# Chunk attention, expert layer, expert layer: chunk form for all attention, wider first loads, and a queue change

## The chip, the cores and the metric

The kernel runs on one core of a Trainium2 chip (trn2). A core has TensorE (matmuls into PSUM, with a weight load of its own), VectorE, ScalarE and GpSimd (called POOL in the profile), and SyncE, which only issues transfers. Each engine runs its own instructions in order; semaphores join them. The metric is the device time of one execution in microseconds; of several runs the median is taken.

## The reference, cut to what matters

```
q, k, v: (4, 8, 768, 64); mem_k, mem_v: (4, 8, 8, 64); float32, q, k and mem_k scaled up
for c in range(24):                       # chunks of 32 queries
    k_ctx = k[:, :, max(0, 32c-16) : min(768, 32c+32+8)]     # v_ctx alike
    scores = (q_c @ concat(mem_k, k_ctx).T) / 8
    a = softmax(scores)                   # subtracts the row's maximum
    out_c = a @ concat(mem_v, v_ctx)
x = out as (3072, 512)
h = x @ w_in (512, 2048); g = h * tanh(log1p(exp(h)));  x = g @ w_out (2048, 512)
h = x @ w_in2;            g = h / (1 + exp(-1.702 h));  y = g @ w_out2
```

The two expert layers have their own weights. The kernel gets arrays as 64-bit floats where they are weights, so a weight arrives as two 32-bit words and is made into one f32 on the chip.

## The kernel before, in words

The 3072 tokens are eight blocks of 384 (`j` = 0 to 7), two for each batch item. For each block attention gives xT, the layer's input with features on partitions; then 16 forward products, one for each slice `f` of 128 hidden columns (L1218), whose results are taken out of PSUM (L1350, L1351) and written to DRAM. Layer 1's second half and layer 2 follow with staged products (seven products in place of eight for each 2 x 2 of halves), into which the change does not reach. From block 1 on every product is three fp32r matmuls (high by high, low by high, high by low); block 0's forward is one plain f32 matmul for each 128 features, because there are no split weights yet.

Attention of blocks 0 and 1 (`EARLY = 2`) is in a windowed form: 96 queries against 120 keys of their neighbourhood and 8 memory keys at a time, with a mask of -3e38 outside each chunk's own keys. `rows_of_heads` loads q, k and v for all eight heads in 256-byte pieces, most of them on SyncE's queue; `turned` has TensorE turn q and k (L761), `quad` makes scores and softmax (L829 to L880), `quad_out` or `oct_out` turns the exponentials (L911, L991) and multiplies by v (L928, L1013). Block 0 is done before the first forward product, block 1 between the forwards of block 0.

Attention from block 2 on is in chunk form: `pair_of_heads` loads q and k for two heads in 128-byte pieces and turns them on VectorE in 32 x 32 squares (L669, L672), `values_of` loads v on POOL's queue, and `duo` does four heads at once: chunk by chunk, 32 queries by 64 keys (8 memory keys among them), scores at L1054, softmax at L1068 to L1088, turn at L1096, values at L1116, and the evictions into xh and xl at L1128 and L1132. Block j's attention stands among the forwards of block j-1.

Layer 1's first weight comes in 16 loads of 0.5 MB, one for each f, in 1-KB pieces (`w_conv`, `w_first`). Each is made into f32 by a drop of the low words (L416 on ScalarE or L419 on VectorE), a shift (L425), a low word (L429) and a sign (L433), and is split into high and low later (`w_cut`; L529, L534).

No engine's order is written by hand. A `Plan` collects operations with a rank and a modelled duration for each engine that could do them, and `issue` lists them in the order of its own modelled time; ties go by rank. So the ranks (`rank`, `base`, `LEAD`, `AHEAD`, `CUT`) and modelled prices (`bus`, the numbers in `load`) set each engine's order and each queue's when the kernel is built. A tile is released when its last reader is done; `Shared`, `Spread` and `Part` place small tiles within large ones.

## Time and profile before

| | us |
|---|---|
| runs before, median of 3 | 1103.59 (1102.69 to 1104.82) |
| the profiled execution, its own time | 1105.13 |
| its span in the trace | 1103.3 |
| TensorE busy | 1079.3 (98%) |
| VectorE busy | 800.3 (73%) |
| ScalarE busy | 555.8 (50%) |
| POOL busy | 98.6 (9%) |
| mean granted TensorE clock, of full speed | 0.998 |

The profile is of one execution. Busy times are of the span; the 1.8 us between span and time lie around the program. PEld is TensorE's weight load, which runs beside its matmuls, and SPq, POOLq and so on are an engine's sequencer, which issues transfers and waits. TensorE is busy almost all the time after the first 40 us, so an average over the span tells little: the stages have to be looked at one by one.

### The profile page before, as it was taken

The page shows a single profiled execution, that of the slowest core. Times are in us where ns is not written, and L with a number is a line of the kernel's source. Part 1 is how long each engine was busy: PE and PEld are TensorE (multiplying, and loading weights), DVE is VectorE, ACT ScalarE, POOL GpSimd, SP SyncE. Part 2 cuts the span into 40 slices and gives each one's busy share as a digit, 9 for nine tenths or more (in the row PEclk, how much of TensorE's full clock was granted, in tenths as well). Part 3 has the DMA queues.
Part 4 walks back from the last instruction along what each step waited for, and adds up shares of the span by engine and source line. Part 5 has one row for each costly group of instructions (what it writes and reads, how often), then busy time and mean ns, then how long its engine had stood idle before and what let it go on. Part 6 is the DMA issues. An engine that isn't in the chain of part 4 may idle for free.

```text
span 1103.3 us, 24808 instructions
## 1 busy us (share of the span) xinstructions
PE 1079.3 (98%) x9642; PEld 1041.1 (94%) x9642; DVE 800.3 (73%) x1456; ACT 555.8 (50%) x1246; POOL 98.6 (9%) x169
## 2 busy tenths in 40 slices
...
GB/s 172 264 241 189 242 247 228 205 250 268 278 276 222 249 175 147 216 212 121 189 172 86 208 260 223 296 227 290 203 265 261 160 106 166 112 133 145 105 165 46
DMA packets 278733, 221.28 MB, mean 201 GB/s; under 512 B 113553, under 2 KB 253868, under 8 KB 278616
## 3 DMA queue, kind: packets, MB, share of 16 engines
...
q14 instruction: 42, 0.34, 0.1%
HBM read 138.33 MB, written 81.26 MB: 199 GB/s over the span
## 4 chain that ended last, share of the span: by engine, by line
PE 78%; DMA 10%; DVE 5%; SPq 4%; issue 1%; ACT 1%; DVEq 0%; ACTq 0%
PE o L1481 9%; PE o L1573 9%; PE h L1218 9%; PE o L1218 8%; PE h L1380 7%; PE o L1380 6%; PE s L1481 6%; PE h L1573 6%; PE h L1481 6%; PE s L1573 5%; SPq L375 4%; PE s L1380 3%; DMA st<-wd 3%; DMA st<-in_moe_w_out_dram 2%; DMA g1d<-ev 1%
## 5 line engine op out<-in xcount | busy, mean ns | idle before, releaser
L1218 PE MATMUL h<-xh,wi 128*128 128x384 f32 x320 | 82.9, 340 | 0.0
L1218 PE MATMUL o<-xh,wi 128*128 128x384 f32 x320 | 82.7, 339 | 0.0
L1218 PEld LDWEIGHTS h<-xh,wi 128*128 128x128 f32 x320 | 57.2, 188 | 0.6
L1218 PEld LDWEIGHTS o<-xh,wi 128*128 128x128 f32 x320 | 57.0, 188 | 0.5
L1218 PE MATMUL h<-xl,wi 128*128 128x384 f32 x160 | 53.7, 336 | 0.0
L1218 PE MATMUL o<-xl,wi 128*128 128x384 f32 x160 | 53.7, 336 | 0.0
L1350 ACT ACTIVATE e<-h 128x384 f32<-128x384 f32 (+2 forms) x47 | 22.4, 477 | 45.4 <-PE h L1573 28.8
L1573 PE MATMUL o<-wo,xh 128*128 128x256 f32 x232 | 43.7, 282 | 0.0
L1563 DVE TENSOR_TENSOR xl<-vt,xh 128x1024 fp32r<-128x1024 f32 x24 | 29.3, 1223 | 19.7 <-ACT xh L1560 18.0
L1563 DVE TENSOR_TENSOR xl<-wi,xh 128x1024 fp32r<-128x1024 f32 x32 | 38.8, 1222 | 5.9 <-ACT xh L1560 5.1
L1481 PE MATMUL o<-xh,wo 128*128 128x256 f32 x224 | 40.5, 282 | 0.0
L1560 ACT ACTIVATE xh<-wi 128x1024 fp32r<-128x1024 f32 x25 | 26.4, 1056 | 23.0 <-DMA wi<-gd 12.4
L375 POOL DMA_DIRECT2D vt<-in_v_dram x50 | 32.2, 648 | 63.3 <-PE o L1116 33.6
L375 POOL DMA_DIRECT2D wo<-in_v_dram x50 | 31.7, 638 | 53.7 <-PE o L1116 51.1
L1464 DVE TENSOR_TENSOR xl<-z,xh 128x1024 fp32r<-128x1024 f32 x24 | 29.2, 1222 | 9.7 <-ACT xh L1460 9.1
L1218 PE MATMUL o<-wo,wi 128*128 128x384 f32 x192 | 36.2, 340 | 0.0
L1573 PEld LDWEIGHTS o<-wo,xh 128*128 128x128 f32 x232 | 36.0, 190 | 0.0
L1218 PE MATMUL h<-wo,wi 128*128 128x384 f32 x192 | 35.7, 339 | 0.0
L1481 PEld LDWEIGHTS o<-xh,wo 128*128 128x128 f32 x224 | 34.6, 190 | 0.0
L1218 PEld LDWEIGHTS h<-wo,wi 128*128 128x128 f32 x192 | 33.2, 188 | 0.2
L1218 PEld LDWEIGHTS o<-wo,wi 128*128 128x128 f32 x192 | 33.0, 188 | 0.4
L1350 ACT ACTIVATE ev<-o 128x384 f32<-128x384 f32 (+2 forms) x31 | 14.5, 469 | 36.7 <-PE o L1573 17.5
...
## 6 DMA issues: line engine op xcount, KB each, us to landing
...
```

What stands on the lines that cost most here:

```text
L375: queue.dma_start(out=o, in_=i)
L1218: nc.tensor.matmul(out=h.get(), lhsT=a[:, c], rhs=b.at(kk), start=(n == 0), stop=(n == KD * len(prods) - 1))
L1350: ("act", act(n, True), lambda: nc.scalar.activation(out=dst(), in_=bank.get(), func=AF.Copy)),
L1380: nc.tensor.matmul(out=bank.get(), lhsT=a, rhs=b, start=(fresh and m == 0), stop=(m == 3 * K2 - 1), skip_group_check=not fresh,)
L1464: add(rank + 0.05, [("dve", dve(n2), lambda gh=gh, gl=gl, src=src: nc.vector.tensor_tensor(out=flat(gl), in0=flat(src), in1=flat(gh), op=A ...
L1481: nc.tensor.matmul(out=bank[:, d, :], lhsT=a, rhs=b[:, p, :], start=(fresh and h == d == p == m == 0), stop=(h == 1 and p == HP - 1 and m ...
L1560: ("act", act(NP * P), lambda: nc.scalar.activation(out=flat(gh), in_=flat(src), func=AF.Copy)),
L1563: add(rank + 0.05, [("dve", dve(NP * P), lambda: nc.vector.tensor_tensor(out=flat(gl), in0=flat(src), in1=flat(gh), op=ALU.subtract))], re ...
L1573: nc.tensor.matmul(out=bank.get(), lhsT=a[:, p], rhs=b, start=(fresh and p == 0 and m == 0), stop=(p == NP - 1 and m == 2), skip_group_che ...
```

## The change

All blocks use the chunk form; the windowed form, its masks and helpers go. Four more things change with it:

- Block 0's q and k come in 1-KB pieces (four rows of 64 floats), q on ScalarE's queue and k on SyncE's, and are turned by TensorE: eight matmuls of 64 x 96 (q) or 64 x 104 (k) with an identity for each pair of heads (L681), taken out of PSUM by strided copies (L695). `WIDE = 0` keeps block 1 on 128-byte pieces on SyncE.
- From block 2 on q's four transfers for each pair of heads go by POOL's queue (`via=NARROW`). v of all blocks does too. Memory values are loaded in even blocks alone, since the odd block finds them in place.
- Layer 1's first weight is loaded for two slices at once, half of the features at a time: still 16 loads of 0.5 MB, but in 2-KB pieces. `Joined` finds a slice's part in the two halves. The first product now needs the first two loads.
- Block 0's results are taken out of PSUM into three tiles in turn (`gh`, `gl`, `ev`), not two.

`attention(j)` is called once at the start of block j-1, its ranks start 4 slices ahead (12 from block 2 on, as before), and the modelled prices of transfers are new. After the change the lines are: drop L430 and L433, shift L439, low L443, sign L447, split L550 and L555; scores L788, softmax L802 to L822, turn L830, values L850, evictions L861 to L866; forward L901, its evictions L1033 and L1034.

```diff
 WARM = 16
-LEAD = 8
+NARROW = 0.64
 SOON = 12
+FIRST = 4
 AHEAD = 6
 CUT = 6
 URGENT = 4
 LANDING = 3.5
-STAGGER = 1.5
 LATE = 3
+WIDE = 0
+LEAD = 2
 TURN = 2.7
 VAL = 7.2
```

```diff
+class Joined:
+    def __init__(self, parts, f):
+        self.parts, self.f = parts, f
+    def __getitem__(self, kk):
+        per = 4 // len(self.parts)
+        part, at = self.parts[kk // per], (2 * (kk % per) + self.f) * 128
+        return part[:, at:at + 128]
```

```diff
-def bus(nbytes, run):
-    return nbytes / 290e3 * (1 if run >= 512 else 1.3 if run >= 256 else 1.8)
+def bus(nbytes, run, soft=False):
+    if soft:
+        return nbytes / 290e3 * (1.07 if run >= 256 else 1.45)
+    return nbytes / 290e3 * (0.8 if run == 2048 else 0.88 if run == 1536 else 1 if run >= 512 else 1.75 if run >= 256 else 1.93)
...
-    T.update(ql=Shared(z0, 0), kl=Shared(z0, TB), mem_t=Shared(z0, TB + 32 * NKB), qT=Shared(z1, 0), kT=Shared(z1, 448))
-    T.update(gh=Shared(z2, 0, TB), aT=Shared(z3, 0, TB))
+    T.update(gh=Shared(z2, 0, TB), aT=Shared(z3, 0, TB), mem_t=Shared(z0, TB + 32 * NKB))
     T.update(tags(ps, h=2, s0=1, s1=1, **{f"o{i}": 1 for i in range(4)}))
     for f in range(NF):
         T.update(tags(sb, **{f"{n}{f}": 1 for n in ("wi", "wo")}))
-    def load(rank, buf, parts, nbytes, run, reads=(), early=False, via=None):
+    w11, w12, w13, w14, w15 = (T[f"wo{i}"].new([P, 2 * DM], F32) for i in range(11, 16))
+    vs = [T["vt"].new([P, 2 * DM], F32) for _ in range(2)]
+    T["ql"] = Spread((z0, 0), (w13, 0))
+    T["kl"] = Spread((z0, TB), (w13, TB))
+    T["qT"] = Spread(*((z, 0) for z in (z1, w15, w11)))
+    T["kT"] = Spread(*((z, TB) for z in (z1, w15, w11)))
+    T["vh"] = Spread(*((z, 0) for z in (w12, w14, *vs)))
+    T["ml"] = Shared(w12, NCH * D)
+    early = [T[f"wi{i}"].new([P, 2 * DM], F32) for i in range(8, 16)]
+    for i, (n, at) in enumerate((("qT", 0), ("kT", TB), ("ql", 0), ("kl", DM))):
+        T[n + "0"] = Spread(*((z, at) for z in early[i // 2 * 4:i // 2 * 4 + 4]))
...
             def go(queue, part=part):
                 o, i = part()
                 queue.dma_start(out=o, in_=i)
 
-            size = bus(nbytes / len(parts), run)
-            ways = [
-                ("sp", 0.475, lambda go=go: go(nc.sync), size),
-                ("pool", 1.2, lambda go=go: go(nc.gpsimd), size),
-            ]
-            add(rank, [("pool", 0.8, *ways[1][2:])] if via else ways if early else ways[:1], reads=reads, writes=[buf])
+            way = ("sp", 0.475, lambda go=go: go(nc.sync), bus(nbytes / len(parts), run))
+            if on == "act":
+                way = ("act", 0.5, lambda go=go: go(nc.scalar), way[3])
+            elif via:
+                way = ("pool", via, lambda go=go: go(nc.gpsimd), bus(nbytes / len(parts), run, True))
+            add(rank, [way], reads=reads, writes=[buf])
```

```diff
-    def w_conv(layer, f, part, rank, after, v, st):
+    def w_conv(layer, f, part, rank, after, v, st, half=None):
         src = w_src[layer, part]
 
         begun.append(fixed())
-        pace_by = begun[-1 - AHEAD:-AHEAD] if (layer, part) == (1, 0) else []
+        pace_by = [] if half is None else begun[-1 - AHEAD:-AHEAD]
 
         st = T[st].new([P, 2 * DM], I32)
         if part == 0:
+            k, c = (KD, 2 * P) if half is None else (KD // 2, 4 * P)
             load(rank - 3, st, [lambda: (
-                st.get().rearrange("p (k c) -> p k c", k=KD),
-                src[:, f * 2 * P:(f + 1) * 2 * P].rearrange("(k p) c -> p k c", p=P),
-            )], P * 8 * DM, 1024, pace_by)
+                st.get().rearrange("p (k c) -> p k c", k=k),
+                src[(half or 0) * k * P:][:k * P, f * 2 * P:f * 2 * P + c].rearrange("(k p) c -> p k c", p=P),
+            )], P * 8 * DM, 4 * c, pace_by)
...
     def w_first(f):
-        if f % 2 == 0:
-            pairs.append(T[f"wo{f // 2}"].new([P, 2 * DM], F32))
-        wi[f] = Part(pairs[-1], f % 2 * DM, DM)
-        w_conv(1, f, 0, f - 1.5, (), wi[f], f"wi{f}")
+        whole = T[f"wo{f // 2}"].new([P, 2 * DM], F32)
+        halves = [Part(whole, i * DM, DM) for i in range(2)]
+        for i in range(2):
+            w_conv(1, f, 0, f - 1.5, (), halves[i], f"wi{f + i}", i)
+            wi[f + i] = (Joined(halves, i),)
 
     def w_cut(f):
-        v = wi[f]
-        wi[f] = split_words(f + CUT, T[f"wi{f}"].new([P, 2 * DM], F32R), 0, DM, v, v.get)
-    pairs = []
+        halves = wi[f][0].parts
+        both = [T[f"wi{f + i}"].new([P, 2 * DM], F32R) for i in range(2)]
+        words = list(zip(*(split_words(
+            f + CUT, [Part(t, i * DM, DM) for t in both], v, v.get) for i, v in enumerate(halves))))
+        for i in range(2):
+            wi[f + i] = [Joined(w, i) for w in words]
```

```diff
+    def wide_pair(j, hp, rank):
+        n, few = 4, LEFT // 4
+        nq, nk = TB // n, NKB * CHUNK // n
+        ql = T["ql0"].new([P, 2, n, D], F32)
+        kl = T["kl0"].new([P, 2, n, D], F32)
+        own = "0" * (j == 0)
+        qT = T["qT" + own].new([P, TB], F32)
+        kT = T["kT" + own].new([P, NKB, BLK], F32)
+        r0 = 2 * hp * S + j * TB
+        k0 = few * (j == 0)
+        lead = LEAD if j else 4
+        load(rank - lead, ql, [lambda: (
+            ql[:nq].rearrange("p h r d -> p h (r d)"), rows(q, r0, [(n, nq), (S, 2)], 0, n * D)
+        )], 2 * TB * D * 4, 1024, on=None if j else "act")
+        if j == 0:
+            add(rank - 4.5, [("dve", 0.25, lambda: nc.vector.memset(kl[:few], 0.0))], writes=[kl])
+        load(rank - lead, kl, [lambda: (
+            kl[k0:nk].rearrange("p h r d -> p h (r d)"), rows(k, r0 + n * k0 - LEFT, [(n, nk - k0), (S, 2)], 0, n * D)
+        )], 2 * NKB * CHUNK * D * 4, 1024)
+        def turn(raw, m, t):
+            for r in range(n):
+                for hh in range(2):
+                    nc.tensor.matmul(
+                        out=t[hh * D:(hh + 1) * D, r * m:(r + 1) * m], lhsT=raw[:m, hh, r], rhs=ident[:m, :m],
+                        start=True, stop=True, tile_position=(0, hh * D),
+                    )
+        for raw, m, to in ((ql, nq, qT), (kl, nk, kT)):
+            t = T["h"].new([P, n * m], F32)
+            add(rank, [("pe", 0.45, lambda raw=raw, m=m, t=t: turn(raw, m, t))], reads=[raw, ident], writes=[t])
+            if to is qT:
+                o, i = qT.get().rearrange("p (t r) -> p t r", r=n), t.get().rearrange("p (r t) -> p t r", r=n)
+            else:
+                o = kT[:, :, :CHUNK].rearrange("p c (t r) -> p c t r", r=n)
+                i = t.get().rearrange("p (r c t) -> p c t r", r=n, t=CHUNK // n)
+            add(rank, [
+                ("act", act(n * m, True), lambda o=o, i=i: nc.scalar.activation(out=o, in_=i, func=AF.Copy)),
+                ("dve", dve(n * m), lambda o=o, i=i: nc.vector.tensor_copy(out=o, in_=i)),
+            ], reads=[t], writes=[to])
```

```diff
+        if j == 0 or j == 1 and hp < WIDE:
+            return wide_pair(j, hp, rank)
         ql = T["ql"].new([P, TB // 32, 32], F32)
         kl = T["kl"].new([P, NKB, 32], F32)
-        qT = T["qT"].new([P, 2 * (GQ + P)], F32)
+        qT = T["qT"].new([P, TB], F32)
...
+        load(rank - (LEAD if j == 1 else 4), ql, qs, P * TB * 4, 128, via=NARROW * (j > 1))
+        load(rank - (LEAD if j == 1 else 4), kl, ks, P * NKB * 128, 128)
         add(rank, [("dve", dve(TB), lambda: nc.vector.transpose(
-            out=qT[:, :TB], in_=ql.get().rearrange("p c d -> p (c d)")
+            out=qT.get(), in_=ql.get().rearrange("p c d -> p (c d)")
         ))], reads=[ql], writes=[qT])
         add(rank, [("dve", dve(NKB * CHUNK), lambda: nc.vector.transpose(out=kT[:, :, :CHUNK], in_=kl.get()))], reads=[kl], writes=[kT])
```

```diff
-            ))
-        load(rank, vt, parts, P * NCH * D * 4, 256, via="pool")
+            if s0 == 0:
+                parts.append(lambda row=i * D + CHUNK, h=h: (
+                    vt[row:row + NM], rows(mem_v, h * NM, [(1, NM), (0, NCH)], 0, D)
+                ))
+        load(rank, vt, parts, P * NCH * D * 4, 256, via=NARROW)
         return vt
...
-    def rows_of_heads(j, gp, rank):
...
-    def turned(j, hp, gp, st, rank):
...
-    def oct_scores(pairs, rank, names):
...
-    def quad(j, hp, gp, heads, rank, given=None, both=None):
...
-    def quad_out(j, hp, gp, vt, rank, names, e):
...
-    def oct_out(j, rank, vt, heads):
```

```diff
+    def attention(j):
+        s0 = j * TB % S
+        base = NF * (j - 1) - (FIRST if j == 0 else 4 if j == 1 else SOON)
+        if s0 == 0:
+            memory_keys(j * TB // S, base)
+        for hp in range(0, H // 2, 2):
+            r0 = base + 4 * hp
+            duo(j, hp, [pair_of_heads(j, hp + i, r0) for i in range(2)], r0)
...
-        ws1 = wi[f] if j else (wi[f],)
+        ws1 = wi[f]
...
                 a, b = ws1[0], x0[j][0]
...
-                        out=h.get(), lhsT=a[:, c], rhs=b.at(kk), start=(n == 0), stop=(n == KD * len(prods) - 1)
+                        out=h.get(), lhsT=a[kk], rhs=b.at(kk), start=(n == 0), stop=(n == KD * len(prods) - 1)
...
-        if j == 0:
-            w_cut(f)
-        t = T[("gh", "gl", "ev")[i % 3] if j else ("gh", "gl")[f % 2]].new([P, TB], F32)
+        if j == 0 and f % 2:
+            w_cut(f - 1)
+        t = T[("gh", "gl", "ev")[i % 3]].new([P, TB], F32)
...
+    attention(0)
     for j in range(NB):
         for f in range(NF):
-            if j == 0:
+            if j == 0 and f % 2 == 0:
                 w_first(f)
-            if j + 1 < NB:
-                attention(j + 1, (f + LEAD) // 2 if j + 1 < EARLY else NQ)
+            if f == 0 and j + 1 < NB:
+                attention(j + 1)
```

The order in which the built kernels issue their instructions, at the places that the prediction speaks of (numbers behind a name count tiles; `x4` is four alike). On SyncE, the transfers around the first weight loads, before: `wi_203` to `wi_283` are the first weight tiles, `wo_162` and `wi_188` hold k and q of block 1, `z_136` block 2's k.

```order
L375 DMA wo_162<-in_mem_k_dram 8x8x64
L375 DMA wi_188<-in_q_dram 96x8x64 x2
L375 DMA wi_203<-in_moe_w_in_dram 128x4x256
L375 DMA wi_207<-in_moe_w_in_dram 128x4x256
L375 DMA wi_219<-in_moe_w_in_dram 128x4x256
L375 DMA wi_229<-in_moe_w_in_dram 128x4x256
L375 DMA wi_234<-in_moe_w_in_dram 128x4x256
L375 DMA z_136<-in_k_dram 32x13x32 x4
L375 DMA wi_283<-in_moe_w_in_dram 128x4x256
L626 DMA z_136<-in_mem_k_dram 8x4x32 x4
```

And after: `wi_92` and `wi_96` hold k of block 0, `z_130` and `wo_173` q and k of block 1's first four heads, `wi_268` and `wi_272` the first two weight loads.

```order
L631 DMA wo_98<-in_mem_k_dram 8x4x32 x4
L388 DMA wi_92<-in_k_dram 100x2x256
L388 DMA wi_96<-in_k_dram 100x2x256
L388 DMA z_130<-in_q_dram 32x12x32 x4
L388 DMA z_130<-in_k_dram 32x13x32 x4
L388 DMA wo_173<-in_q_dram 32x12x32 x4
L388 DMA wo_173<-in_k_dram 32x13x32 x4
L388 DMA wi_268<-in_moe_w_in_dram 128x2x512
L388 DMA wi_272<-in_moe_w_in_dram 128x2x512
```

The weight loads stand behind block 1's narrow pieces of four heads, where they stood behind block 1's q and k in the windowed form.

On ScalarE, around the first forward product, before (`xh` is block 0's input to it; its last part is written from `o_585`):

```order
L416 ACTIVATE wo_469<-wi_207 128x512
L963 ACTIVATE xh<-o_507 128x192
L529 ACTIVATE wi_532<-wo_469 128x512
L768 ACTIVATE z_152<-h 128x448
L416 ACTIVATE wo_544<-wi_219 128x512
L860 ACTIVATE e,sm<-e,mx 96x128 x4
L416 ACTIVATE wo_544<-wi_229 128x512
L860 ACTIVATE e,sm<-e,mx 96x128 x4
L963 ACTIVATE xh<-o_585 128x192
```

And after, where `s_665` and `o_667` hold block 0's last four heads and `wo_641` is the third pair's weight:

```order
L430 ACTIVATE wo_641<-wi_302 128x512
L430 ACTIVATE wo_641<-wi_310 128x512
L550 ACTIVATE wi_649<-wo_506 128x512 x2
L550 ACTIVATE wi_658<-wo_590 128x512 x2
L550 ACTIVATE wi_715<-wo_641 128x512
L861 ACTIVATE xh<-s_665 128x384
L861 ACTIVATE xh<-o_667 128x384
L550 ACTIVATE wi_715<-wo_641 128x512
L836 ACTIVATE z_425<-s_728 128x384
```

Block 0's last evictions now stand behind two drops and five splits of weights.

On TensorE, around the first forward product, before (L911 to L991 are turns and values of the windowed form):

```order
L911 MATMUL o_572<-ident,ev 128x96 x4
L928 MATMUL o_585<-z_267,vt 64x96 x4
L1218 MATMUL h<-xh,wo_469 128x384 x4
L991 MATMUL s_625<-ident,e 128x96 x4
L1218 MATMUL h<-xh,wo_469 128x384 x4
L991 MATMUL s_658<-ident,e 128x96 x4
L1218 MATMUL o_663<-xh,wo_544 128x384 x4
L1218 MATMUL o_684<-xh,wo_544 128x384 x4
```

And after:

```order
L850 MATMUL o_667<-z_425,vt 64x32
L830 MATMUL s_728<-ident,e 128x128 x3
L901 MATMUL h<-xh,wo_506 128x384 x8
L830 MATMUL o_780<-ident,e 128x128 x3
L901 MATMUL o_788<-xh,wo_590 128x384 x4
L901 MATMUL o_811<-xh,wo_590 128x384 x4
L850 MATMUL s_830<-z_425,wo_98 64x32
```

The first turn of block 1 (`s_728`) now stands ahead of the first forward, and two forwards run before the next turn.

## Rows read from the trace of the kernel before

**Rows 1.** Stages: window, length, then busy us (instructions) of PE, PEld, DVE, ACT, POOL; clock, DMA share, GB/s.

```profile
0.00:39.07 39.07, 28.50 (x272) 23.67 (x272) 24.79 (x134) 24.71 (x99) 5.94 (x14) 0.96 1.01 201
39.07:94.21 55.14, 53.79 (x371) 33.41 (x369) 51.60 (x150) 39.52 (x124) 3.58 (x7) 1.00 0.88 230
94.21:379.00 284.79, 279.39 (x3626) 269.44 (x3625) 175.01 (x435) 138.74 (x466) 89.04 (x149) 1.00 0.89 245
379.00:1103.30 724.30, 717.58 (x5379) 714.60 (x5378) 548.87 (x740) 352.79 (x561) 0.00 (x0) 1.00 0.58 181
```

**Rows 2.** TensorE's timeline: start, us, engine, line, operation, shapes, count, [idle before, releaser].

```profile
39.07 2.85 PE L1218 MATMUL h<-xh,wo 128*128 128x384 f32 x8
...
45.40 5.35 PE L1218 MATMUL o<-xh,wo 128*128 128x384 f32 x16
50.59 0.25 PE L761 MATMUL h<-ident,wi 96*128 96x96 f32 x1
```

**Rows 3.** Busy time of PE, PEld in 94.21:320.51 by line: L1054, L1096, L1116.

```profile
94.21:320.51 226.30, 13.87 (x1056) 11.63 (x1056) 1.00 0.92 245
...
94.21:320.51 226.30, 11.88 (x72) 8.53 (x72) 1.00 0.92 245
...
94.21:320.51 226.30, 19.14 (x1152) 17.89 (x1152) 1.00 0.92 245
```

**Rows 4.** TensorE's longest waits, 94 to 330: waited for, us in total, times, longest.

```profile
PE s L1096 <- DVE e L1088: 1.5, 1, 1.5
PE s L1054 <- issue: 1.3, 2, 1.0
PE o L1096 <- ACT z L1350: 1.0, 1, 1.0
```

**Rows 5.** VectorE's timeline, a weight conversion.

```profile
44.33 0.68 DVE L429 SCALAR_TENSOR_TENSOR wo<-wi,wo 128x512 int32<-128x512 int32 x1
44.93 0.41 DVE L425 TENSOR_SCALAR wo<-wo 128x512 int32<-128x512 int32 x1
```

**Rows 6.** Timelines of VectorE and ScalarE, softmax in chunk form.

```profile
91.91 0.52 DVE L1069 TENSOR_REDUCE mx<-s 128x6 f32<-128x384 f32 x1
...
93.24 0.31 ACT L1076 ACTIVATE e<-s,mx 128x64 f32<-128x64 f32 x1 [0.82 <-DVE mx L1071]
...
95.00 0.34 ACT L1076 ACTIVATE e<-o,mx 128x64 f32<-128x64 f32 x1
```

**Rows 7.** TensorE's timeline, the warm-up and block 1's values.

```profile
1.36 6.67 PE L1631 MATMUL o<-ident 128*128 128x128 f32 x32 [1.36 <-POOL ident masks.py:199]
...
60.96 0.88 PE L1013 MATMUL s<-z,vt 128*64 128x96 f32 x16
```

**Rows 8.** DMA from 20 to 25, 30 to 35 and 76 to 95: packets, rate, sizes.

```profile
DMA packets 3904, 0.98 MB, mean 196 GB/s; under 512 B 3904, under 2 KB 3904, under 8 KB 3904
...
DMA packets 1738, 1.74 MB, mean 349 GB/s; under 512 B 51, under 2 KB 1737, under 8 KB 1737
...
DMA packets 11999, 2.77 MB, mean 146 GB/s; under 512 B 11157, under 2 KB 11933, under 8 KB 11997
```

**Rows 9.** POOL's issues at L375, 94 to 330 (min/median/max ns); two timeline rows at 125 us.

```profile
L375 POOL DMA_DIRECT2D vt<-in_v_dram x46: 626/642/696, 93.7 to 267.9; - x46
...
DMA to landing us min/median/max: 2.6/4.7/7.9
...
125.42 1.27 POOL L375 DMA_DIRECT2D wo<-in_v_dram  x2
...
125.69 0.61 DVE L425 TENSOR_SCALAR v<-v 128x512 int32<-128x512 int32 x1
```

**Rows 10.** TensorE's timeline, two alike transposes; the stretch 10 to 20, columns as rows 1.

```profile
17.72 0.85 PE L911 MATMUL o<-ident,e 96*128 96x96 f32 x4
...
21.11 0.55 PE L911 MATMUL o<-ident,ev 96*128 96x96 f32 x4
...
10.00:20.00 10.00, 5.49 (x54) 4.61 (x52) 6.21 (x40) 5.17 (x23) 0.00 (x0) 0.88 1.10 164
```

480 lines of the change are left out of this document (63 added, 417 removed).

## Prediction, made before the changed kernel was run

> **What bounds the kernel now.** I read the table of stages first [rows 1]. From 94.21 us, the start of block 1's forward, to the end TensorE is busy 279.39 of 284.79 and 717.58 of 724.30 us, at a granted clock of 1.00. Nothing there can win time unless it takes matmuls away or a wait of TensorE. In the first 39.07 us TensorE is busy 28.50, VectorE 24.79 and ScalarE 24.71: nobody is the bound alone. It is a chain from block 0's queries to its scores, softmax, values and the first product. From 39.07 to 94.21 TensorE is busy 53.79 of 55.14 and VectorE 51.60 of 55.14, so both are nearly full. What the change can win lies before 94.21, and the end moves by what the start of block 1 moves, as long as TensorE then stays as full as it is.
>
> The second view is TensorE's own timeline [rows 2]. The first forward product starts at 39.07. Two f-slices of block 0 take from 45.40 to 50.59, 5.19 us, so 2.6 for one slice and 41.5 for 16. Of the 55.14 us this leaves 13.6 for attention: all of block 1 in its windowed form, the waits in it, and the first scores of block 2. The third view is the waits of TensorE after 94 us [rows 4]: the three longest are 1.5, 1.3 and 1.0, and with smaller ones I count 5 us until 330 us.
>
> **The change, part by part.**
>
> *Attention of block 1 in chunk form (gain).* Prices come from the stretch in which six blocks run in that form already [rows 3]: 1056 score matmuls are 11 groups of 96, so 13.87 / 11 = 1.26 us; 72 turns are 24 of three, 0.50 each; 1152 matmuls of values are 12 groups, 1.60 each. Busy time of a group runs into what follows: 45.40 shows 5.35 busy where the next starts 5.19 later [rows 2], so 0.16 comes off each: 1.10, 0.34 and 1.44. In the new order the scores of block 1's first four heads stand ahead of the first forward; behind it stand one group of scores, four turns and two groups of values: 1.10 + 4 x 0.34 + 2 x 1.44 = 5.3 us. In the old kernel 13.6 less the first scores of block 2 (1.1) stood there, 12.5. TensorE is so relieved of 12.5 - 5.3 = **7.2 us** (with the busy times in full 6.4, and the gain at least 6). The turns, values and scores of block 2 that now also stand before block 1's start are only moved: they go from the one side of that start to the other. VectorE, which is 94% busy there, loses the evictions and the mask operations of the windowed form, so it doesn't take TensorE's place: its cover is the 16 weight conversions, each about 2.1 us in four operations and the split's one or two.
>
> *The start of the first forward (the cost side).* The new order is a chain I can price row by row. The 16 warm-up matmuls end at 8.0 [rows 7], as now. Then stand three head pairs' turns by TensorE, six groups of eight matmuls of 96 or 104 columns. No such group exists now; the nearest row is eight f32 matmuls of 96 columns in 0.88 us busy (16 records, two for each f32 matmul), 0.85 taken [rows 7]. If instead each cost what a fresh weight and a 384-column product cost (0.65 per matmul and 2.6 for four, rows 2), it would be 1.4 for the group; without the reload it may be 0.4. So the turns end at 8.0 + 6 x 0.85 = 13.1 (10.4 to 16.4), the first scores at 14.2. Then VectorE carries 28 operations up to its first weight operation: four reductions and three normalisations at 0.5, four transposes and one eviction at 0.5, and small ones; a reduction is 0.52 busy [rows 6]. I sum 8.0 and reach 22.2. ScalarE runs beside it: six exponentials from 93.24 to 95.00 are 1.76 us [rows 6], four such groups 7.0, from 15.6 to 22.7, so neither waits much for the other.
>
> From there VectorE has, in the new order, the conversion of five weight loads (two drops, five shifts, five low words, five signs), the last normalisation of block 0 and block 1's first softmax, all ahead of what frees ScalarE. Conversion prices: low word 0.60 (44.33 to 44.93, 0.08 under its busy 0.68), shift 0.41 less the like, 0.34 [rows 5], drop as the shift, sign as the low word: 7 x 0.34 + 10 x 0.60 = 8.4; the softmax and copies between them 4.5. That gives 35.1. On ScalarE the evictions of block 0's last four heads, which the first forward reads, stand behind the split of the fifth load: 0.55 + 2 x 0.4 = 1.4, so 36.5. POOL issues its 25 transfers of v in the same time; a VectorE operation beside such an issue took 0.61 where the like takes 0.41 [rows 5, 9], and for some six such meetings I add 1.2. The first forward would start at 37.7.
>
> *POOL's chain.* Behind those 25 transfers POOL copies the memory keys into block 1's k, which gates block 1's first scores and so VectorE. In the built program transfer n waits for transfer n-8. An issue is 0.64 us [rows 9], eight are 5.1 us, and a transfer lands after 2.6 to 7.9 us, median 4.7 [rows 9]. At 4.7 the copy comes at 1.6 + 25 x 0.64 = 17.6 and holds nobody; at 7.9 it comes at 1.6 + 3 x 7.9 + 0.6 = 26, where VectorE wants the scores at about 22.8: up to 4 us late. I take 1.0, nearer to the median row. First forward at **38.7** then, against 39.07 now.
>
> *The clock.* TensorE has little work from about 24 to 38.7. In 10 to 20, busy 5.49 of 10 us, its granted clock was 0.88: 2.4 us of the ten at 1.2 GHz, the rest at 2.4. Four transposes at 17.72 took 0.85 and the like at 21.11 0.55 [rows 10], so the low level lasted up to 1.1 us beyond 20: some 3.5 us of work at half speed, 1.7 us lost. I take the same for the first slice or two after the pause (0 if the clock holds). Now the slices run at full speed from the first, 2.85 [rows 2]. So this part costs 38.7 + 1.7 - 39.07 = **1.3 us**.
>
> *Weights in 2-KB pieces.* Now 1-KB pieces move at 349 GB/s, against 196 for 256-B pieces and 146 for mostly 128-B ones [rows 8]; 0.5 MB takes 1.5 us. Larger pieces are no slower; a bound from below is nothing gained. What must land before the fifth load is done: 1.57 MB of q and k in 1 KB (4.5 us), 0.8 MB of v in 256 B (4.1), 0.8 MB in 128 B (5.5) and 2.6 MB of weights (7.5): 21.6 us, from about 1 us on. The fifth load is then here at 23 and used by ScalarE at about 28. I cost it at nothing; if the pieces gained nothing and v delayed it by its 4.1 us, it would still be in time.
>
> *q from block 2 on by POOL.* 16 issues more in each block. POOL has 24 issues in an even block and, since memory values are now loaded in even blocks alone, 16 in an odd one: 40 and 32 now, 40 x 0.64 = 25.6 us. A block lasts 284.79 / 7 = 40.7 [rows 1], so it is covered, at nothing; SyncE loses 16 issues. The cover ends at 40.7 / 40 = 1.02 us for an issue.
>
> The sum: -7.2 + 1.3 = -5.9 us; 1105.13 for the profiled execution becomes 1099.2. The runs' median, 1103.59, is 1.5 below the profiled one, so I say **1098**.
>
> **The rivals.**
> *B, the copies and weights come late.* POOL's copy at 26 delays the first forward by 3.4 beyond the forecast, 42.1. For it: the DMA engines are full in the first 39 us (share 1.01, rows 1). Against: block 0's q and k, 1.57 MB, move in 4.5 us at 349 GB/s where 256-B pieces at 196 took 8.0 [rows 8]. It gives 1101.4 to 1104: no difference that can be told (a measurement here tells 0.2%, 2.2 us, from none).
>
> *C, POOL becomes the bound (slower).* From block 2 on q waits in POOL's queue behind v, whose transfers wait for the buffers that the earlier values release. If an issue costs over 1.02 us, or a landing over 8.2 us (eight in flight), even blocks are longer than their products. Were an issue to wait out the VectorE operation beside it, 0.64 + 0.61 [rows 9], 40 would take 50 us, 9.3 too many, in blocks 2, 4 and 6: +28, so 1126. Against it: 46 issues took 626 to 696 ns with VectorE busy 175 of 284.79 us, and the pair at 125.42 and 125.69 [rows 9] shows the VectorE operation as the longer one, not the issue. The Trainium skill, "SBUF — State Buffer", section "SBUF: two separate sides", has the rule that speaks for this rival: a transfer issued from GpSimd can't get its descriptors written while VectorE runs a two-port operation, and its section "A bandwidth-pool intuition that's wrong (but worth ruling out)" gives about 620 ns alone and 3100 ns overlapped; by that figure POOL's queue would be three times over a block's length. The trace so far does not bear it out.
>
> *D, more is won.* The clock holds (-1.7), the copy is never late (-1.0), and part of the 5 us of later waits goes, since SyncE's queue is shorter and k comes earlier: 1090 to 1095. For it: the longest, 1.5, is for a softmax on VectorE that could start sooner. Against: VectorE gets no less work there.
>
> *E, the change doesn't do what it says:* the order shows that it does; I give it nothing.
>
> **How the numbers follow.** A, the forecast, 1095 to 1101: 0.55. B: 0.18. C: 0.10. D: 0.17. The range leaves out C and the ends of B and D: 1091 to 1104. Faster by over 0.2% (under 1101.4): A, D and a little of B, 0.76; within 0.2%: most of B, 0.13; slower: C and a little more, 0.11.
>
> **What the profile of the changed kernel should show.** The first forward at 37 to 40 us, with a granted clock under 1 just before and its two first slices longer than 2.85 each; six groups of turns between 8 and 13; the last weight operation before it on VectorE near 35. Block 1's first product should start at about 91.5: 5.9 earlier, and 3.2 later for the turns, values and scores of block 2 (2 x 0.34 + 1.44 + 1.10) that now stand ahead of it. POOL's issues stay near 0.64 us, and TensorE's waits until 330 near 5. I am wrong if the first forward is after 42, if block 1 starts later than 95, or if TensorE waits for q or v in blocks 2 to 7 by more than now.

## The result: 0.6% slower

The changed kernel takes 1110.27 us (median; 1109.92 to 1111.45) beside 1103.38 for the kernel before: a ratio of 1.0063, with a 95% interval of 1.0045 to 1.0080. Forecast were 1098 and a gain. The profiled execution took 1111.45 us, against a sum of 1099.2 for it: 12.3 us to explain.

The table by stages of the changed kernel, the answer to [rows 1] (window, length, then busy us (instructions) of PE, PEld, DVE, ACT, POOL; clock, DMA share, GB/s). The cuts are the first forward product, block 1's first product, and the last forward of block 7.

```profile
0.00:46.70 46.70, 28.74 (x655) 25.52 (x656) 24.23 (x73) 23.88 (x96) 23.10 (x45) 0.72 0.95 211
46.70:109.00 62.30, 57.00 (x723) 35.54 (x722) 47.69 (x114) 30.16 (x108) 41.37 (x69) 0.94 0.92 223
109.00:382.20 273.20, 272.89 (x3425) 265.22 (x3425) 171.29 (x420) 127.19 (x414) 102.92 (x168) 1.00 0.83 244
382.20:1109.70 727.50, 719.47 (x5380) 715.58 (x5379) 546.41 (x732) 356.51 (x569) 0.00 (x0) 1.00 0.58 180
```

Cut at the same events (block 1's first product that reads xl), the kernel before has 39.1, 55.8, 283.9 and 724.5. So the start lost 7.6 us, block 0's forward lost 6.5 (3.2 of it, block 2's first steps that now stand ahead of the cut, was forecast), blocks 1 to 7 won 10.7, and the rest lost 3.0: 6.4 in all.

Where TensorE stood is read from its timeline in the first 110 us (start, us, engine, line, operation, shapes, count, [idle before, releaser]), the answer to [rows 2, 7]:

```profile
13.31 1.28 PE L681 MATMUL h<-ident,wi 104*64 104x104 f32 x16 [1.72 <-DMA wi<-in_k_dram]
...
14.53 0.31 PE L788 MATMUL s<-wi 64*32 64x64 f32 x1
...
32.27 0.31 PE L850 MATMUL s<-z,wo 64*64 64x32 f32 x1 [3.77 <-issue]
...
46.05 0.90 PE L830 MATMUL s<-ident,e 128*128 128x128 f32 x3 [5.53 <-ACT xh L861]
46.74 7.59 PE L901 MATMUL h<-xh,wo 128*128 128x384 f32 x16
54.49 5.33 PE L901 MATMUL o<-xh,wo 128*128 128x384 f32 x16
...
101.45 0.24 PE L788 MATMUL s<-wo 64*32 64x64 f32 x1 [2.56 <-issue]
```

The turns ended at 14.5 (forecast 13.1), behind 1.72 us of waiting for k. The first scores ran from 14.53 to 16.51, at a granted clock of 0.50 (forecast: done by 14.2). Then TensorE stood 3.77 us in the middle of block 0's values with "issue" beside it: it waited for nothing that the profile shows. The first forward started at 46.74, and its first two slices took 7.4 us where two take 5.3 later. At 101.45 stands a second such gap, in block 2's scores.

TensorE's waits until 104 us and, after the "...", from 104 to 330 us, the answer to [rows 4] (engine, line, waited for: us in total, times, longest):

```profile
PE s L830 <- ACT xh L861: 6.1, 2, 5.5
PE s L850 <- issue: 3.8, 1, 3.8
PE s L788 <- issue: 3.3, 2, 2.6
PE s L830 <- DVE mx L805: 2.3, 1, 2.3
PE s L788 <- POOL wo L646: 2.0, 1, 2.0
PE h L681 <- DMA wi<-in_k_dram: 1.7, 1, 1.7
...
PE o L830 <- DVE e L822: 0.3, 1, 0.3
```

From 104 us on 0.3 us is left of the 5.3 that stood from 94 on before.

What the first gap did to VectorE and, after the fourth "...", ScalarE, from their timelines (columns as above):

```profile
16.48 0.09 DVE L802 MEMSET s<- 32x32 f32 x1 [3.86 <-PE s L788]
...
20.52 0.61 DVE L733 STREAM_TRANSPOSE z<-z 128x416 f32<-128x416 f32 x1 [1.88 <-DMA z<-in_k_dram]
...
27.58 0.43 DVE L433 TENSOR_SCALAR wo<-wi 128x512 f32<-128x512 f32 x1 [0.51 <-DMA wi<-in_moe_w_in_dram]
...
36.81 0.56 DVE L837 COPY z<-o 128x384 f32<-128x384 f32 x1 [5.05 <-PE o L830]
...
44.32 1.29 ACT L550 ACTIVATE wi<-wo 128x512 fp32r<-128x512 f32 x2 [1.44 <-DVE wo L447]
...
45.52 0.47 ACT L861 ACTIVATE xh<-s 128x384 f32<-128x384 f32 x1
```

VectorE reached its first weight operation at 27.58, not at 22.2. Then it waited 5.05 us for the last turn of block 0, that of its last four heads, which stands in TensorE's queue behind the values that the gap had stopped. Most of its conversions came only after that, the splits on ScalarE waited for them (L550), and the eviction that the first forward reads (L861, 45.52) stands behind the splits.

The granted clock in two stretches, the answer to [rows 10] (columns as in the table by stages):

```profile
24.00:51.00 27.00, 15.64 (x307) 12.31 (x308) 20.69 (x53) 15.56 (x60) 10.09 (x17) 0.50 0.97 262
102.00:106.00 4.00, 4.00 (x8) 2.16 (x7) 1.80 (x5) 2.83 (x20) 3.76 (x6) 0.57 0.44 97
```

From 24 to 51 us the clock was at its lower level, 1.2 GHz, with TensorE busy 15.64 of 27 us; in the kernel before it was 1.00 over the same 27 us, with TensorE busy 22.72. Behind the second gap it fell again.

POOL's issues of q and v from 94 to 330 us, beside [rows 9] (engine, operation, count: ns min/median/max; last, the time from issue to landing in us):

```profile
L388 POOL DMA_DIRECT2D vt<-in_v_dram x46: 527/628/931, 94.3 to 289.5; - x46
L388 POOL DMA_DIRECT2D z<-in_q_dram x40: 615/617/888, 98.0 to 256.8; - x40
L388 POOL DMA_DIRECT2D wo<-in_q_dram x40: 617/617/783, 100.4 to 271.3; - x40
L388 POOL DMA_DIRECT2D wo<-in_v_dram x40: 617/656/676, 103.5 to 267.6; - x40
...
DMA to landing us min/median/max: 2.1/4.1/8.3
```

### The profile page after: what moved, and what is told of

Read it like the earlier page. It is cut to its first block, busy times and chain, and to the rows that moved or that the text cites. A ratio compares the mean times of both kernels' runs of the same rounds, so it can differ in the third digit from the quotient of the medians.

```text
span 1109.7 us, 25759 instructions
## 1 busy us (share of the span) xinstructions
PE 1078.1 (97%) x10178; PEld 1041.9 (94%) x10178; DVE 789.6 (71%) x1338; ACT 537.7 (48%) x1186; POOL 167.4 (15%) x281
## 3 DMA queue, kind: packets, MB, share of 16 engines
q8 instruction: 80, 1.31, 0.5%
## 4 chain that ended last, share of the span: by engine, by line
PE 84%; DMA 8%; DVE 3%; SPq 1%; issue 1%; ACT 1%; POOL 0%; ACTq 0%; DVEq 0%; POOLq 0%
PE o L901 12%; PE h L901 12%; PE o L1164 9%; PE o L1256 8%; PE h L1063 8%; PE o L1063 7%; PE s L1164 6%; PE h L1164 6%; PE h L1256 5%; PE s L1256 5%; PE s L1063 3%; PE s L850 2%; SPq L388 1%; DMA wo<-in_v_dram 1%; DMA st<-wd 1%
## 5 line engine op out<-in xcount | busy, mean ns | idle before, releaser
L901 PE MATMUL h<-xh,wi 128*128 128x384 f32 x320 | 83.1, 341 | 0.0
L901 PE MATMUL o<-xh,wi 128*128 128x384 f32 x320 | 82.9, 340 | 0.0
L901 PEld LDWEIGHTS h<-xh,wi 128*128 128x128 f32 x320 | 57.1, 188 | 0.6
L901 PEld LDWEIGHTS o<-xh,wi 128*128 128x128 f32 x320 | 57.0, 188 | 0.6
L901 PE MATMUL o<-xl,wi 128*128 128x384 f32 x160 | 53.8, 336 | 0.0
L901 PE MATMUL h<-xl,wi 128*128 128x384 f32 x160 | 53.8, 336 | 0.0
L388 POOL DMA_DIRECT2D vt<-in_v_dram x66 | 42.5, 649 | 50.4 <-PE o L850 45.2
L388 POOL DMA_DIRECT2D wo<-in_v_dram x66 | 42.1, 645 | 40.4 <-PE o L850 34.6
L1033 ACT ACTIVATE e<-h 128x384 f32<-128x384 f32 (+2 forms) x47 | 22.4, 476 | 46.2 <-PE h L1256 29.6
L1033 ACT ACTIVATE ev<-o 128x384 f32<-128x384 f32 (+2 forms) x32 | 15.1, 471 | 46.1 <-PE o L1256 18.9
L810 ACT ACTIVATE e<-s,mx 128x64 f32<-128x64 f32 x90 | 26.9, 321 | 19.1 <-DVE mx L805 17.0
L901 PE MATMUL h<-wo,wi 128*128 128x384 f32 x192 | 36.1, 340 | 0.0
L901 PE MATMUL o<-wo,wi 128*128 128x384 f32 x192 | 35.5, 341 | 0.0
L1256 PE MATMUL o<-wo,xl 128*128 128x256 f32 x116 | 32.8, 283 | 0.7 <-DVE xl L1246 0.7
```

The source lines that it names most:

```text
L388: queue.dma_start(out=o, in_=i)
L810: nc.scalar.activation(out=e[:, g, i], in_=s[hh][:, g, i], func=AF.Exp, scale=scale, bias=mx[:, g, i:i + 1], accum_out=sm[:, g, i:i + 1],)
L901: nc.tensor.matmul(out=h.get(), lhsT=a[kk], rhs=b.at(kk), start=(n == 0), stop=(n == KD * len(prods) - 1))
L1033: ("act", act(n, True), lambda: nc.scalar.activation(out=dst(), in_=bank.get(), func=AF.Copy)),
L1256: nc.tensor.matmul(out=bank.get(), lhsT=a[:, p], rhs=b, start=(fresh and p == 0 and m == 0), stop=(p == NP - 1 and m == 2), skip_group_che ...
```

## The experiments

All kernels but e1 and e12 are the changed kernel with one edit or several; those two are edits of the kernel before. Code cuts show the line that matters, not the whole edit. In the table, "idle" is the length of the stretch from the first forward to block 1's first product less TensorE's busy time in it, and "clock" is that length times one less the granted clock, an estimate of the time lost by the lower level (a little too high where TensorE stood idle at that level, since "idle" counts that too). Both are from the rows by stages of each profile. For e9, e10 and e13 the profiled execution was the fastest, 4 to 6 us under the median, so their stages are flattered by as much; that of e3 was the slowest, 2 us over.

| kernel | median us | ratio (95%) | first forward at | to block 1 | idle | clock | blocks 1 to 7 |
|---|---|---|---|---|---|---|---|
| before | 1103.4 | 1 | 39.1 | 55.8 | 1.4 | 0 | 283.9 |
| changed | 1110.3 | 1.0063 (1.0045, 1.0080) | 46.7 | 62.3 | 5.3 | 3.7 | 273.2 |
| e1_block1 | 1122.3 | 1.0175 (1.0140, 1.0211) | 40.1 | 64.4 | 6.8 | 5.8 | 288.0 |
| e2_memk | 1110.4 | 1.0057 (1.0034, 1.0079) | 45.6 | 65.6 | 7.1 | 5.2 | 272.3 |
| e3_1kb | 1105.7 | 1.0011 (0.9997, 1.0025) | 48.9 | 54.7 | 0.6 | 1.6 | 276.3 |
| e5_ahead3 | 1107.7 | 1.0042 (1.0020, 1.0065) | 43.3 | 58.9 | 5.8 | 4.7 | 279.3 |
| e6_1kb_a2 | 1125.5 | 1.0195 (1.0180, 1.0211) | 41.9 | 88.3 | 19.9 | 11.5 | 270.4 |
| e7_hot | 1110.0 | 1.0061 (1.0037, 1.0085) | 47.9 | 64.6 | 6.0 | 7.1 | 272.6 |
| e8_q_sp | 1115.4 | 1.0103 (1.0077, 1.0129) | 46.2 | 60.0 | 3.1 | 4.2 | 284.4 |
| e9_1kb_a4_hot | 1104.7 | 1.0019 (1.0004, 1.0035) | 44.7 | 50.5 | 2.8 | 0 | 277.7 |
| e10_light | 1105.2 | 1.0024 (0.9999, 1.0048) | 42.2 | 59.1 | 2.9 | 4.1 | 272.4 |
| e11_1kb_a4 | 1104.1 | 1.0012 (0.9996, 1.0028) | 47.6 | 51.1 | 2.0 | 1.0 | 278.2 |
| e12_before_qpool | 1101.9 | 1.0001 (0.9982, 1.0019) | 39.0 | 55.0 | 1.0 | 0 | 281.4 |
| e13_later | 1102.8 | 1.0000 (0.9984, 1.0016) | 41.3 | 58.4 | 2.8 | 1.8 | 273.1 |
| e14_apart | 1106.4 | 1.0025 (1.0010, 1.0041) | 43.3 | 65.7 | 7.6 | 5.9 | 272.5 |
| e15_later2k | 1109.3 | 1.0044 (1.0031, 1.0057) | 41.1 | 69.2 | 7.5 | 9.7 | 273.7 |

The table answers one question by itself. In the nine kernels whose stretch "to block 1" holds the same 722 or 723 matmul records (changed, e2, e3, e7, e8, e10, e13, e14, e15) it lasts 54.7 to 69.2 us; less idle and clock it lasts 51.5 to 53.8. Forecast were 41.5 for 16 slices and 9.6 of attention; with 0.7 for the two products of block 1 ahead of the cut that is 51.8. So the count of the work was nearly right, and everything else in that stretch is TensorE standing still or running at 1.2 GHz.

### Chunk form alone

```diff
-EARLY = 2
+EARLY = 1
```

> The kernel before with block 1 alone in chunk form (EARLY = 1); block 0, the weights' pieces and all else as before. Theory (the chunk form's saving on TensorE is real, and the changed kernel lost it again ahead of the first forward): the first forward stays at 39 us, block 1's attention costs 7 us less of TensorE, 1096 to 1098. Rival (the chunk form brings its own empty times of TensorE, the changed kernel shows 0.8, 2.0 and 2.6 us ahead of score groups after its first forward): most of the gain is gone, 1100 to 1103.

Chunk form for block 1 in the old order cost 18 to 19 us instead of winning 7. From 40 to 104 us TensorE waited 3.9 us for an eviction on VectorE and had a clock of 0.91:

```profile
40.10:104.50 64.40, 57.59 (x625) 34.69 (x624) 47.80 (x111) 28.25 (x97) 27.86 (x47) 0.91 0.93 200
```

So the saving on TensorE does not come by itself. The chunk form has many more small instructions (625 matmuls here, 373 before), and the stretch in which they stood took 8.6 us longer. The other stretches lost too: 1.0 up to the first forward, 4.1 in blocks 1 to 7 and 3.4 behind them; why is not shown.

### What makes the first forward late

mem_k of block 0 by POOL, so that SyncE's queue is shorter:

```diff
-                    nc.sync.dma_start(
+                    (nc.sync if b else nc.gpsimd).dma_start(
```

> The changed kernel with block 0's four small memory-key transfers on POOL's queue ahead of v, so that SyncE issues k of all four head pairs at once. Theory (a chain from block 0's k and memory keys: SyncE held k of pairs 2 and 3 until 7.65 us, VectorE waited for memory keys until 11.8, first weight operation at 27.6): k and memory keys are there by about 9, the first weight operation comes 3 to 5 us earlier, first forward at 42 to 44 instead of 46.7, 1105.5 to 1108. Rival (TensorE's empty 3.8 us at 28 to 32 and the weights set the first forward): nothing moves by more than 1 us, 1109.5 to 1111.

The first forward came 1.1 earlier and the time did not move. Fewer weight loads ahead (`AHEAD`):

```diff
-AHEAD = 6
+AHEAD = 3
```

> The changed kernel with at most three weight loads ahead of their conversion in place of six (AHEAD = 3). In the built order block 0's last evictions on ScalarE then stand behind two splits instead of five, and VectorE converts three loads ahead of them instead of five. Theory (the conversions that stand ahead of the last evictions are a link of the chain): first forward 3 to 5 us earlier, 42 to 44, 1105 to 1108; TensorE's empty time at 28 also shrinks if the queued weight loads cause it. Rival (the chain is v and k alone): first forward stays at 46 to 47, and weights come late after it, 1110 to 1114.

The first forward came 3.4 earlier, but from there to the end of block 7 took 338.2 us where it took 335.5; the total fell by about 2.5, less than the two intervals can tell from none. The gap in block 0's values was still 3.2 us. In the next two the splits wait until block 0's forward of the same slice is done (`split_words` reads `pace[f + 1]` also), mem_k goes by POOL, and e13 has the 1-KB pieces of e3 below as well, with `AHEAD = 4`:

```diff
-            reads=[src], writes=[hi],
+            reads=[src, *when], writes=[hi],
```

> Four edits of the changed kernel together: 1-KB pieces, at most four loads ahead, block 0's memory keys on POOL ahead of v, and the split of a first weight only after block 0's forward with it has been issued (block 1 is the first that needs the split). In the built order no split stands ahead of block 0's last evictions, and a forward stands between the last values and the last scores before block 1. Theory (the first forward is set by what stands ahead of those evictions and by the late piece of TensorE's program; after it, the empty times come where two groups of small products follow each other): first forward at 40 to 43, block 1 starts 51 to 55 us behind it, total 1097 to 1101, faster than before by 3 to 6 us. Rival (the half clock and the late pieces cost the same wherever the order puts the work): 1102 to 1106, no faster than before.

> 2-KB pieces as in the changed kernel and six loads ahead, with block 0's memory keys on POOL ahead of v and the splits only after block 0's forward, as in the run before with 1-KB pieces. Theory (the piece size costs nothing; the order of conversions ahead of the first forward does): first forward at 41 to 43, total within 2 us of that run, 1101 to 1105. Rival (2-KB pieces cost by themselves, since the first product needs two loads converted and large pieces hold up what else the DMA engines carry): first forward at 43.5 or later, 1106 to 1109.

Both bring the first forward to 41.1 to 41.3, so the splits ahead of the last evictions, with mem_k (1.1 in e2), were some 5 us of its delay. But e13 is only level with the kernel before, and e15 (2-KB pieces) is hardly better than the changed kernel: it gives back more than that in idle time and clock (17.2 us together, 9.0 in the changed kernel). Its theory, a total within 2 us of e13, failed: it is 6.5 above. The clock is at the lower level until 53 us:

```profile
24.00:53.00 29.00, 20.29 (x267) 13.90 (x268) 19.23 (x51) 9.42 (x38) 12.04 (x20) 0.50 0.99 225
```

An early first forward is not worth its microseconds: e15 starts at 41.1 and ends at 1109, e3 at 48.9 and ends at 1106.

### 1-KB pieces again

Each slice's weight in one load of 1-KB pieces, as before the change (cut; the load itself and `w_cut` follow suit):

```diff
-            w_conv(1, f, 0, f - 1.5, (), halves[i], f"wi{f + i}", i)
-            wi[f + i] = (Joined(halves, i),)
+            v = Part(whole, i * DM, DM)
+            w_conv(1, f + i, 0, f + i - 1.5, (), v, f"wi{f + i}", -1)
+            wi[f + i] = (Whole(v),)
```

> The changed kernel with layer 1's first weight in 1-KB pieces again, one load for each slice; all else as changed. Theory (the piece size is not what makes the first forward late): first forward within 1.5 us of 46.7, a little earlier since the first slice needs one load and not two, 1108.5 to 1111. Rival (loads of 2-KB pieces crowd out what TensorE needs at 28 to 32, where it stood empty for 3.8 us in the middle of a group of values): that empty time goes, first forward at 42 to 43, 1105 to 1107.

This gave back about 5 us, though the first forward came 2.2 later. The gain is in the stretch to block 1:

```profile
48.90:103.60 54.70, 54.15 (x723) 34.12 (x723) 43.94 (x107) 26.99 (x96) 35.50 (x60) 0.97 0.93 232
```

Idle time fell from 5.3 to 0.6 and the loss by the clock from 3.7 to 1.6: the gap of 2.56 us in block 2's scores is gone, and so is the wait of 2.0 for POOL's copy, while the gap of 3.77 in block 0's values stands as before. With it three more, to push the same way: fewer loads ahead, and idle products to hold up the clock.

```diff
-AHEAD = 6
+AHEAD = 2
```

> 1-KB pieces of the first weight as in the run before, and at most two loads ahead of their conversion (AHEAD = 2), so that hardly any weight traffic stands beside block 0's values. Theory (TensorE's empty time at 28 to 32 is a 16-KB piece of its own program that comes late through DMA engines full of weights): the empty time in the middle of block 0's values falls from 3.8 to under 1.5 us, the first forward comes at 41 to 42; later the conversions come late, total 1104 to 1109. Rival (the empty time has nothing to do with the weights' traffic): it stays at 3 to 4 us, first forward at 43 to 44.

e6 starts its forwards at 41.9, then waits 6.2 us for weights and 10.5, in five places, with "issue". Its 88.3 us to block 1 hold 380 more matmul records too, since block 2's steps went on while the slices stood. Two loads ahead are too few. The theory on the gap in block 0's values failed: it was 3.2 us here, and the rival's 3 to 4 us came true.

```diff
+        if j == 0 and hp0:
+            hot(r0 + VAL + 0.01, HOT[1], o[0])
```

> The changed kernel with 16 idle products of the identity added on TensorE (six behind the scores of block 0's last four heads, ten behind their values; results unused), which cost 2.5 and 4.2 us at full clock and lie in waits. Theory (TensorE ran block 0's values and the first two forwards at half clock, since it had little to do): the clock is back at the first forward or soon behind, the first two slices take 5.3 to 6.3 us instead of 7.4, total 1107 to 1109. Rival (the extra products only delay the first forward, the clock does not follow): 1111 to 1114.

Sixteen idle products (six behind block 0's second scores, ten behind its values) hardly shortened the first two slices (7.02 us busy, 7.59 without them) and won nothing, although the clock did move: it was back at full speed from 44.8 us, some 6.5 earlier than without them, but fell again from 48.2 to 51.6. e9 is 1-KB pieces with `AHEAD = 4` and the idle products, e11 the same without them:

> Three edits together: 1-KB pieces, at most four loads ahead (AHEAD = 4) and the 16 idle products. Theory (late conversions ahead of block 0's last evictions, and the clock, are the two things that can be won back): first forward at 42 to 44, the first slices near 2.7 each, total 1100 to 1104. Rival (what is won at the first forward is lost again in waits before block 1, as with AHEAD = 3): 1105 to 1108.

> 1-KB pieces and at most four loads ahead, without the idle products of the run that had all three. Theory (order ahead of the last evictions is what was won there, and the idle products hold the clock): first forward at 42 to 44 here, first slices at 3.3 to 3.7 us each, total 1105 to 1108, slower than with the products. Rival (the products do nothing): 1103 to 1105, as with them.

The totals agree within their intervals: what the idle products are worth is less than this can tell. On the clock they do act, as the 4.3 us from the first forward of e9 and the 4.4 us from that of e11 show:

```profile
44.70:49.00 4.30, 4.30 (x16) 2.58 (x15) 4.30 (x11) 1.66 (x3) 3.98 (x7) 1.00 1.03 306
```

```profile
47.60:52.00 4.40, 4.40 (x12) 2.52 (x11) 4.37 (x12) 1.39 (x3) 3.92 (x7) 0.71 1.03 320
```

Neither kernel is faster than the one before.

### What "issue" is

The instruction records up to the gap at 28.5 us, in the changed kernel, in e3 and in e7 (one row of each; columns as in the table by stages):

```profile
0.00:28.53 28.53, 20.75 (x471) 18.31 (x471) 11.13 (x38) 13.02 (x58) 17.31 (x35) 0.86 0.95 186
```

```profile
0.00:27.66 27.66, 19.87 (x471) 17.69 (x471) 12.33 (x43) 13.00 (x58) 17.25 (x35) 0.88 1.00 193
```

```profile
0.00:28.22 28.22, 22.09 (x472) 19.61 (x472) 10.83 (x39) 12.92 (x58) 17.07 (x34) 0.87 1.01 183
```

Matmuls and weight loads together make 942, 942 and 944, although e7 has other instructions there, idle products having been put in ahead. The other gap of the changed kernel, at 98.9, stands behind 1351 + 1351 = 2702 records, 1760 or 7 x 251 later. So the gap belongs to a place in TensorE's instruction stream, not to an operation. Counted with the records of TensorE's sequencer, the four gaps with "issue" of the changed kernel (0.63, 3.77, 0.78 and 2.56 us) stand at records 705, 961, 1729 and 2753: 256, 768 and 1024 apart, all whole numbers of 256. Of the 56 such waits in the 16 kernels 55 stand at these places or further ones of the same grid; the odd one is 0.76 us in e7. The page of the changed kernel has a queue named "instruction" with 80 packets and 1.31 MB, 16 KB each; TensorE has 2 x 10178 records, 254 for each of 80, as the kernel before has 2 x 9642 for 76. And each of the 55 waits ended 1.3 to 1.8 us after such a packet had landed. So these waits are for the next piece of TensorE's own program. The queues from 20 to 29.8 us and, after the "...", from 29.8 to 31.2 us (packets, MB, share of 16 engines):

```profile
q1 hardware_dynamic: 3440, 2.03, 86.7%
q0 software_dynamic: 326, 0.47, 19.7%
...
q1 hardware_dynamic: 274, 0.53, 101.1%
q8 instruction: 1, 0.02, 4.8%
```

TensorE began the piece ahead of the gap at 20.30. From 20 to 29.8 us no piece of its program moved, while the DMA engines were full, first of narrow pieces of q, k and v, then of weights; the next one moved from 29.8 to 30.9, and TensorE resumed at 32.27. A group of 48 scores or values is 192 records, three quarters of a piece, in 1.1 to 1.5 us, where a forward slice is 16 records in 2.6 us. If a piece waits behind weights, light weights should let it through. In e10 the first six loads bring an eighth of their bytes, and VectorE zeroes the rest (cut):

```diff
+            few = c if half is None or f > 5 else 64
+            if few < c:
+                add(-29, [("dve", 1.2, lambda: nc.vector.memset(st.get(), 0))], writes=[st])
```

> The changed kernel with the first six weight loads cut to an eighth of their bytes (the rest of those tiles is set to zero by VectorE in its idle first microseconds), so the first weight is wrong in part; the order on TensorE, ScalarE and SyncE is that of the changed kernel. Theory (a 16-KB piece of TensorE's program waits behind the weights in the DMA engines; it began to land at 29.9 us although the piece before was begun at 20.3): the empty time of 3.8 us at 28 shrinks to under 1.5 us, and with it the first forward comes 3 us or more earlier, at 42 to 44; total 1105 to 1108. Rival (the piece is late for another reason, the weights are not in its way): the empty time stays at 3 to 4 us; weights that land earlier move the first forward by under 1.5 us, total 1109 to 1111.

DMA from 25 to 35 us in e10, then in the changed kernel:

```profile
25.00:30.00 5.00, 1.94 (x102) 1.49 (x100) 4.56 (x18) 4.80 (x31) 0.00 (x0) 0.94 0.72 115
30.00:35.00 5.00, 4.51 (x134) 3.81 (x119) 4.53 (x16) 3.88 (x26) 0.00 (x0) 0.50 0.44 79
```

```profile
25.00:30.00 5.00, 3.35 (x116) 2.74 (x116) 3.77 (x15) 2.26 (x14) 0.00 (x0) 0.50 1.07 313
30.00:35.00 5.00, 2.36 (x79) 2.22 (x79) 1.77 (x5) 0.88 (x2) 0.20 (x1) 0.50 1.05 377
```

The DMA share falls to 0.72 and 0.44, and the gap of 3.77 is gone, as the theory said. TensorE's waits until 48 us in e10:

```profile
PE h L684 <- DMA wi<-in_k_dram: 6.8, 1, 6.8
PE s L833 <- DVE mx L808: 2.6, 1, 2.6
...
PE o L791 <- issue: 0.5, 1, 0.5
```

But the piece did not come earlier. The queues in e10 from 25.7 to 29.8 us and, after the "...", from 29.8 to 31.2 us:

```profile
q1 hardware_dynamic: 3368, 0.43, 67.3%
...
q1 hardware_dynamic: 264, 0.03, 14.0%
q8 instruction: 1, 0.02, 5.7%
```

It landed at 31.1, in the changed kernel at 30.9. What changed is when TensorE needed it: it had waited 6.8 us for k, behind the zeroing, and came to that place in its program at 32.7, not at 28.5. So e10 does not show that weights hold a piece up, and other runs speak against it as the only cause: with three and with two loads ahead the gap was still 3.2 us (e5, e6), and in e14 below, with all the weights as they were, the same piece moved at 22.9. The first forward starts 4.5 earlier; how much of that is the gap and how much the lighter loads was not separated. The clock is at 0.50 here too, so lighter loads do not cure that. And the gap in block 2's scores stands, where the order on TensorE is that of the changed kernel:

```profile
93.79 0.24 PE L791 MATMUL s<-wo 64*32 64x64 f32 x1 [2.85 <-issue]
```

The other way to help a late piece is to need it later. In e14 one forward slice stands between block 2's first values and its second scores:

```diff
-        add(r0 + SCORE, [("pe", COSTS, scores)], reads=reads, writes=s)
+        add(r0 + SCORE + 0.5 * (j == 2 and hp0 > 0), [("pe", COSTS, scores)], reads=reads, writes=s)
```

> The changed kernel with one number added to one rank: block 2's second group of scores is put half a slice later. In the built order one forward slice then stands between block 2's first values and these scores, which followed each other directly; the order on POOL is the same, and on the other engines a few rows move. Theory (a group of small products uses up a piece of TensorE's program faster than the next one lands; with a forward between them the next one is there): the empty time of 2.6 us at 99 to 101 goes or falls under 0.8, the half clock behind it goes too, 3 to 5 us off, total 1105 to 1107.5. Rival (the piece is late wherever the scores stand): the empty time stays over 2 us, 1109 to 1111.

97 to 110 us in e14, then in the changed kernel, and the scores at which the gap had been:

```profile
97.00:110.00 13.00, 12.91 (x231) 8.87 (x230) 5.67 (x18) 4.72 (x20) 11.96 (x21) 1.00 0.94 186
```

```profile
97.00:110.00 13.00, 10.44 (x182) 7.12 (x174) 6.08 (x19) 4.65 (x26) 11.83 (x20) 0.87 0.81 175
```

The gap and the lower clock behind it are gone. The piece came no faster: it landed 3.2 us after TensorE had begun the piece ahead of it, in the changed kernel 3.0. But TensorE now took 4.6 us over that piece, not 1.8. This is a cure that the traces show: long products between the groups give the next piece time.

What the cure is worth is less clear. The median fell by 3.8 of the 6.9 us, but in the two profiles block 1 starts at 109.0 in both: e14's first forward came 3.4 earlier, since in this run the gap in block 0's values is not there, and a new wait of 5.0 us for ScalarE stands behind it. Of the 5.1 us between the profiles 4.4 lie behind block 7, where the kernels do not differ.

In e3 a slice stands between the same two groups as well, so the 1-KB pieces moved the order. Whether the size of the pieces costs something by itself stays open: e15 and e13, 6.5 us apart, differ in it, but also in `AHEAD`.

### q by POOL

```diff
-        load(rank - (LEAD if j == 1 else 4), ql, qs, P * TB * 4, 128, via=NARROW * (j > 1))
+        load(rank - (LEAD if j == 1 else 4), ql, qs, P * TB * 4, 128, via=0)
```

> The changed kernel with q of blocks 2 to 7 back on SyncE's queue. Theory (q on POOL is not the loss; TensorE's waits from 109 us on are 0.3 us in the changed kernel against 5.3 before): the waits of blocks 2 to 7 come back in part, total 1110 to 1114. Rival (POOL's queue holds q and v back, as the 2.0 us wait for a copy on POOL at 79 us suggests): 1106 to 1108.

Put back on SyncE, q costs 4 to 5 us. Blocks 1 to 7 take 11 more, the other stretches together 6 less (the row of blocks 1 to 7, then TensorE's longest waits in it):

```profile
106.20:390.60 284.40, 275.67 (x3424) 267.60 (x3424) 170.70 (x420) 127.78 (x417) 58.58 (x99) 0.99 0.82 235
```

```profile
PE s L830 <- ACT e L810: 5.5, 1, 5.5
PE h L901 <- issue: 1.9, 1, 1.9
```

If that is so, q on POOL's queue should help the kernel before (cut; memory values in even blocks only go with it):

```diff
-        load(rank - 4, ql, qs, P * TB * 4, 128)
+        load(rank - 4, ql, qs, P * TB * 4, 128, via="pool")
```

> The kernel before with one part of the change alone: q of blocks 2 to 7 on POOL's queue and memory values in even blocks only; blocks 0 and 1 stay in the windowed form. Theory (this part is a gain by itself: TensorE's waits in blocks 1 to 7 were 5.3 us before and 0.3 in the changed kernel, and 8.7 us of idle time came back with q on SyncE): 4 to 8 us faster than before, 1096 to 1100, the first forward unmoved at 39. Rival (the waits went because blocks 0 and 1 are in chunk form, not by the queue): 1102 to 1105.

It does not, measurably: TensorE's waits from 94 to 330 us went from 5.3 to 2.5 and the ratio is 1.0001. The queue is worth something only in the changed order. That SyncE carries more narrow pieces there (block 1's) would fit, but is only argued.

## Why the prediction was wrong

**The first forward: 38.7 forecast, 46.7 measured.** This is the step that failed, by 8.0 of the 12.3 us.
- The first scores were done at 16.5, not at 14.2: the turns waited 1.72 for k, and the scores took 2.0 us at half clock where 1.10 was summed. VectorE so began 2.3 late.
- VectorE's 28 operations were sized rightly (8.0; it was busy 7.57 from 14.53 to 27.58), and it did not wait for ScalarE. But the sum had no wait for loads in it, and VectorE waited 3.4 us for block 1's q and k (1.88 the longest) and for the weight. Its first weight operation was 5.4 late.
- TensorE's gap was not foreseen. It held up block 0's values and the turns of its last four heads behind them, and VectorE waited 5.05 for the last of these. The remaining steps took 2.4 less than the 16.5 summed, about as much as the two allowances for POOL in them (1.2 and 1.0): 5.4 + 5.05 - 2.4 = 8.0. In e14, where this gap did not come, the first forward stood at 43.3.
- POOL's copy, for which 1.0 was put in and on which rival B rested, ran at 23.32 for block 1's first keys and was not the cause. It did cost 2.0 us at 79.5, ahead of a group of scores.

**Chunk form on TensorE: -7.2.** Of this 1.4 was the old kernel's idle time, which leaves 5.8 of work. Less idle and clock the stretch is 54.4 before and 53.3 - 3.2 in the changed kernel (3.2 for block 2's steps): 4.3 saved, and 3.8 to 6.1 over the nine kernels. The step that failed is to price the groups by [rows 3] alone. Those are groups that stand between long fp32r products at a clock of 1.00, so that the next piece of the program has time to come. In blocks 0 and 1 the groups stand close together, and 5.3 us of idle time (1.4 before) and 3.7 us of clock came on top (forecast for the clock: 1.7 in the first slices, which took 2.1 more there; the rest stands behind the gap of 2.56). So -4.3 + 3.2 + 3.9 + 3.7 = 6.5, what the stretch lost. The sign was there: in [rows 4] 1.3 us is "issue" at scores, and so is a further row of that view,

```profile
PE o L1054 <- issue: 0.7, 1, 0.7
```

which the prediction counted among the waits without asking what they were.

**Later waits.** Rival D's part came true: 5.3 to 0.3 us after block 1's start. With it, first forward to the end of block 7 is 335.5 us against 334.2 by the forecast's steps (339.7 - 7.2 + 1.7). That this is close is luck: 8.8 more than forecast before block 1's start and 7.5 less behind it, of which 5.1 is idle time and 2.4 is not explained.

**The rest of the program** lost 3.0 where nothing was changed: TensorE was busy 1.7 longer and idle 1.3 longer. Neither is explained. Over the kernels here this part ran from 722.9 to 727.9. So 8.0 + 1.3 + 3.0 = 12.3.

**2-KB pieces at nothing:** ahead of the first forward VectorE waited 0.5 us for a load and ScalarE 2.1, so the loads themselves cost little. But with 1-KB pieces and the order that comes with them the kernel was about 5 us faster (e3). The forecast had no term for a moved order. That the order accounts for all of it, and the size for none, is not shown.

**q by POOL at nothing** was right in its mechanism and rival C fell: issues took 527 to 931 ns, median 617 to 656, never the 1.02 us from which C would have decided, and landings took 4.1 us in the median. The Trainium skill, "SBUF — State Buffer", section "A bandwidth-pool intuition that's wrong (but worth ruling out)", gives about 3100 ns for a transfer issued from GpSimd that overlaps a VectorE copy. No issue here took as long; which VectorE operations beside them are of that kind, no row shows. In the changed order the queue is worth 4 to 5 us.

What stays open: why the clock stays low longer in some orders (until 51 to 53 us in the changed kernel and e15). The rows show that it fell in the stretch of small, interrupted groups and came back some way into the forward products, with idle products in e9 just ahead of them, not more. Also not settled is what a program piece waits behind: in the 13 kernels here with block 0 in chunk form the piece for the place behind 942 records (944 with the idle products) began to move at 27.8 to 30.5 us, whatever was done to the weights, but for e14. There, with nothing changed ahead, it moved at 22.9. There was no gap behind 942 records, but small ones behind 442 (0.80 us) and 1190 (0.58). No version here beats the kernel before by more than the measurement can tell.
